# Fourier filter, routed experts and a dense block in one kernel: a weight unit every five steps, 15 leading blocks, half of the splits on GpSimd

## The chip, the cores and the metric

The kernel runs on one core of a Trainium2 chip. The metric is device time of one execution in microseconds (us). Three executions of the kernel before took 4052.21, 4054.33 and 4055.38 us; the median is 4054.33 us. Engines are named as the profile names them: PE is TensorE (matmuls; PEld are its weight loads), DVE is VectorE, ACT is ScalarE, POOL is GpSimd, SP is SyncE, which here issues DMAs. Each engine runs its own instructions in order, and semaphores tie them to each other.

## The reference

Three stages follow each other, all in fp32:

```python
X = np.fft.rfft(x, axis=1)                              # x: 8 x 3072 x 256
y = np.fft.irfft(X * (filt_r + 1j * filt_i), n=3072, axis=1)
x = y.reshape(24576, 256)
e = argmax(x @ w_gate, axis=1)                          # one of 8 experts per token
out[mask] = gate[mask] * (relu(x[mask] @ w1[e]) @ w2[e])   # 256 -> 1024 -> 256
h = out @ w_in                                          # 256 -> 2048, weights in float64
g = h if h >= 1, 0 if h <= -1, else (h + 1)**2 / 4
result = g @ w_out                                      # 2048 -> 256, weights in float64
```

To reach fp32 accuracy the matmuls of the last two stages run as three products: every operand is split into a rounded part ("hi") and the remainder ("lo"), and hi*hi, hi*lo and lo*hi are added up.

## The kernel before

The first stage (class `Conv`) transforms, filters, transforms back, writes the rows `y` to memory and routes each token to its expert. It ends at about 740 us. The other two stages are class `Ffn`, and this is where the change lies.

Tokens are gathered by expert into blocks: 41 wide blocks of 512 tokens and 21 narrow ones of 256. A block `j` has 8 parts, one step `("b", j, f)` each. A b step of a wide block is 12 matmuls on PE: six with w1 into `h` (`b_in`, L844) and, three steps later (`LAG = 3`), six with w2 into the sums `y` (`b_out`, L857). Between the two, ACT rounds `h` to `hh` and DVE computes the remainder `hl` (L854). The dense block works in chunks of 512 tokens, 16 steps `("c", c, f)` each. `run` (L986) writes all steps into one list. The first `8 * LEADERS + 12` steps are b steps alone (the lead: 13 blocks and a half); from there on, eight b steps are spread among the 16 c steps of each chunk until the wide blocks are used up. Narrow blocks are spread over every second chunk.

`plan` (L1044) sets, counted in steps ahead of a block's own step, when its work is issued: `gather` issues indirect DMAs on POOL, token numbers 26 steps ahead, rows 16 ahead (first argument of `early`, plus 7); `scale` (L825) multiplies the rows by their gate on DVE; `take` (L831) transposes one half of the rows on PE into the one PSUM bank `xt`, after which ACT copies it to `xh` and DVE writes the remainder `xl`. With `early = (9, 7, 4)` the scale stands 9 steps ahead of the block, the first half 7 and the second half 4. The second half's transposes write the bank that the first half's `xl` reads. `load_w` loads a quarter of a block's expert weights into one of three `raw` buffers, by a DMA on SP; `split_w` (L796) has ACT copy 128x512 weights to `wh`, and a step later `lo_part` (L776, the subtraction is at L778) writes the remainder `wl`. Which engine does that is decided at L801: in the lead DVE for every step, later DVE for even `f` and POOL for odd `f`.

`decode` (L738) converts the float64 weights of the dense block, 16 units of 128x512 numbers, during the last part of the lead. A unit loads `d_raw` on SP; seven DVE and two ACT instructions follow over several steps (a `yield` ends the part of a step). A new unit starts every 4 steps, and the first starts 69 steps ahead of the end of the lead. When the sums of a block are full, `b_end` (L872) has ACT copy them to `cyh` and DVE write `cyl`.

`play` (L1057) issues, for each step: the matmuls of `b_in` and the ACT half; then the remainders due (`fill`); then `hl`; then everything in `todo` for the next step (gathers, scale, transposes, loads, weight copies, decode); then `b_out` of three steps ago. Steps below are counted from the first b step, which is step 0.

Of the kernel before, what the change touches and what calls it, by code (L numbers as in the profile page):

```python
# [13 lines left out]
ACTF = mybir.ActivationFunctionType  # L14
ALU = mybir.AluOpType
# [16 lines left out]
NS = 21  # L32
NBLK = NW + NS
SURE = NBLK - 4
LEADERS = 13
WARM = 44
SPLIT_FROM = 3
NX = 7
# [647 lines left out]
class Ffn:  # L686
# [6 lines left out]
    def __init__(self, ctx, tc, a, st):  # L693
# [6 lines left out]
        self.rawp, self.wp = pool("c_raw", 3), pool("c_w", 7)  # L700
        self.idp, self.idl, self.rowp = pool("c_id", 12), pool("c_il", LEADERS), pool("c_row", 8)
        self.xp, self.hp, self.y1p, self.cyp = pool("c_x", 2), pool("c_h", 4), pool("c_y1", 1), pool("c_cy", 2)
# [35 lines left out]
    def decode(self, n):  # L738


        nc, V, pool = self.nc, self.nc.vector, self.dp
        q, k = divmod(n, 4)
        if k < 2:
            src = self.a["win"].bitcast(I32)[128 * k : 128 * k + 128, 1024 * q : 1024 * q + 1024]
            hi, lo = (t[:, k, 512 * q : 512 * q + 512] for t in (self.winh, self.winl))
        else:
            i = 4 * q + 2 * (k - 2)
            src = self.a["wout"].bitcast(I32)[128 * i : 128 * i + 256].rearrange("(t p) c -> p t c", p=128)
            hi, lo = (t[:, i : i + 2].rearrange("p t d -> p (t d)") for t in (self.woh, self.wol))
        raw = pool.tile([128, 512, 2], I32, name="d_raw")  # L750
        dst = raw.rearrange("p n w -> p (n w)")
        nc.sync.dma_start(dst if k < 2 else dst.rearrange("p (t c) -> p t c", t=2), src)
        yield
        yield
        h, l = raw[:, :, 1], raw[:, :, 0]
        e = pool.tile([128, 512], I32, name="d_e")
        m = pool.tile([128, 512], I32, name="d_m")
        f = m[:].bitcast(FP32)
        V.tensor_scalar(out=e, in0=h, scalar1=20, scalar2=0x7FF, op0=ALU.logical_shift_right, op1=ALU.bitwise_and)
        nc.scalar.activation(e, e, ACTF.Relu, bias=self.ebias[:, 0:1], scale=2.0**23)  # L760
        V.tensor_scalar(out=l, in0=l, scalar1=8, scalar2=0xFFFFFF, op0=ALU.logical_shift_right, op1=ALU.bitwise_and)
        yield
        V.tensor_scalar(out=m, in0=h, scalar1=0xFFFFF, scalar2=None, op0=ALU.bitwise_and)
        V.scalar_tensor_tensor(out=e, in0=h, scalar=-(2**31), in1=e, op0=ALU.bitwise_and, op1=ALU.bitwise_or)
        yield
        V.scalar_tensor_tensor(out=f, in0=l, scalar=2.0**-24, in1=m, op0=ALU.mult, op1=ALU.add)
        V.scalar_tensor_tensor(out=f, in0=f, scalar=2.0**20, in1=e[:].bitcast(FP32), op0=ALU.add, op1=ALU.mult)
        nc.scalar.copy(hi, f)
        yield
        self.lo_part(f, hi, lo, True)  # L770
# [14 lines left out]
    def at(self, i, fn, when=None):  # L785
        (self.todo if when is None else when).setdefault(max(i, self.now), []).append(fn)
# [9 lines left out]
    def split_w(self, j, f, i):  # L796
        q, t = divmod(f, 2)
        hi = self.wp.tile([128, 4, 128], F32R, name="wh")
        lo = self.wp.tile([128, 4, 128], F32R, name="wl")
        src = self.RAW[j, q][:, 512 * t : 512 * t + 512].rearrange("p (a b) -> p a b", b=128)  # L800
        self.halves(i, src, hi[:], lo[:], f % 2 == 0 or i < self.lead)  # L801
        self.W[j, f] = (hi, lo)

    def gather(self, j, more):
# [3 lines left out]
        if not more:  # L808
            pool, name = (self.idl, "idl") if j < LEADERS else (self.idp, "ids")
            ids = self.IDS[j] = pool.tile([128, 4, 2], I32, name=name)  # L810
# [61 lines left out]
    def b_end(self, j, acc, n):  # L872
# [4 lines left out]
        for k in range(2):  # L877
            nc.scalar.copy(hi[:, k], acc[k])
            nc.vector.tensor_tensor(out=lo[:, k], in0=acc[k], in1=hi[:, k].bitcast(FP32), op=ALU.subtract)
        if LEADERS <= j < NW:  # L880
            self.CY[j] = (hi, lo, self.rows(self.IDS.pop(j)))
# [104 lines left out]
    def run(self):  # L986
        self.now = -self.LEAD
        sure = SURE
        chunks = [*range(LEADERS, NW), *range(LEADERS), *range(NW, self.nch)]
        wide = [("b", j, f) for j in range(NW) for f in range(8)]  # L990
        narrow = [[("b", j, f) for f in range(8)] for j in range(NW, sure)]
        lead = self.lead = 8 * LEADERS + 12
        steps, wide = wide[:lead], wide[lead:]
        for m, c in enumerate(chunks):
            more, wide = wide[:8], wide[8:]
            if m >= 2 and m % 2 == 0 and narrow:
                more[4:4] = [None, *narrow.pop(0), None]
            n = max(8, len(more))
            for f in range(16):
                steps += [("c", c, f), *filter(None, more[f * n // 16 : (f + 1) * n // 16])]  # L1000
        assert not wide and not narrow
        pos = {x: i for i, x in enumerate(steps)}
        at = self.at
        fork = pos["c", self.nch - 3, 5]
        at(fork - 16, self.load_used)

        for c in range(self.nch):
            if c < LEADERS or c >= NW:
                at(pos["c", c, 0] - 7, lambda c=c: self.load_c(c))
            for t in range(4 if c < self.nch - 1 else 0):  # L1010
                at(pos["c", c, 15] + 2 + self.LAG + t, lambda c=c, t=t: self.scatter(c, t))
        for j in range(sure):
            p = [pos["b", j, f] for f in range(8)]
            if j <= LEADERS + 1:
                self.plan(p, j, soon=j == 0)
            else:
                self.plan(p, j, ahead=6, lead=8, early=(13, 11, 6))
        for n in range(16):
            d = self.decode(n)
            for k in range(7):  # L1020
                at(lead - 69 + 4 * n + k, lambda d=d: next(d, None))
        at(lead - 1, self.dense)

        for i in self.play(steps):
            if i == fork:
                self.rest(sure)
            yield i
# [13 lines left out]
                pass  # L1041
        self.todo, self.fill, self.now = keep

    def plan(self, p, j, ahead=3, lead=4, soon=0, early=(9, 7, 4)):  # L1044

        at, i = self.at, p[0] - soon
        at(p[0] - 26, lambda: self.gather(j, False))
        at(p[0] - early[0] - 7, lambda: self.gather(j, True))
        at(i - early[0], lambda: self.scale(j))
        for k in range(2):  # L1050
            at(i - early[1 + k], lambda k=k: self.take(j, k, i - early[1 + k] + 1))
        for q in range(4):
            at(p[2 * q] - ahead - lead, lambda q=q: self.load_w(j, q))
        for f in range(8):
            at(p[f] - ahead, lambda f=f: self.split_w(j, f, p[f] - ahead))
# [129 lines left out]
```

## Time and profile before

| what | value |
|---|---|
| profiled execution | 4052.3 us |
| its span in the trace | 4050.5 us |
| PE busy | 3906.5 us (96%) |
| DVE, ACT, POOL busy | 2230.3, 2006.8, 2236.0 us |
| mean granted clock of PE over the span | 0.984 of 2.4 GHz |

A share of the whole span says little here, since the kernel has stages: the first stage up to about 580 us, its tail mixed with the lead up to about 740 us, the lead with the decoded weights up to 1010.7 us, the chunks with wide blocks up to about 2950 us, and the rest. A step can be found in the trace by its six matmuls of L850; step 0 starts at 578.5 us, step 47 at 738.3 us, and the 116 steps of the lead have ended by 1010.7 us.

### The profile page before, as it was taken

What the parts mean: (1) busy time and instruction counts of PE and PEld (TensorE: products, weight loads), DVE (VectorE), ACT (ScalarE), POOL (GpSimd) and SP (SyncE); (2) the same over time, 40 slices, a digit from 0 to 9 for tenths busy, and PEclk for the clock granted to TensorE, in tenths of its full rate; (3) what the DMA queues carried; (4) which work ended last, traced back from release to release, by engine and by line L of the source; (5) the groups of instructions that cost most, each with busy time, mean ns of one, the idle gap of its engine ahead of it and who ended that gap; (6) DMA issues with size and microseconds to landing.
All of it is one profiled execution on the core that took longest, in us unless ns stands there. A gap on an engine that the chain in (4) does not pass through costs nothing. (4 is left out here: it accounts for less than half of the span.)

```text
span 4050.5 us, 63427 instructions
## 1 busy us (share of the span) xinstructions
PE 3906.5 (96%) x23852; PEld 3337.2 (82%) x23852; DVE 2230.3 (55%) x3621; ACT 2006.8 (50%) x3592; POOL 2236.0 (55%) x2112
## 2 busy tenths in 40 slices
PE   8999999888999999999999999999999999999999
PEld 5766667666888888888888888888888889888888
DVE  4577766766555554554555555555545454444444
ACT  4767654444444454444444444444444444444444
POOL 5878773211555555555555555555555555555555
PEclk9999989988999999999999999999999999999999
DMA  9878764443112221221221221221211111111010
GB/s 282 253 223 229 204 186 138 139 151 136 42 61 59 70 59 60 65 68 57 62 73 52 62 72 56 60 70 55 60 61 59 55 38 51 48 36 33 32 43 17
DMA packets 227992, 361.94 MB, mean 89 GB/s; under 512 B 35456, under 2 KB 143264, under 8 KB 227680
## 3 DMA queue, kind: packets, MB, share of 16 engines
q1 hardware_dynamic: 202400, 306.38, 24.8%
q0 software_dynamic: 25056, 51.36, 4.5%
q8 instruction: 190, 3.11, 0.3%
q14 instruction: 122, 1.00, 0.1%
q10 hardware_dynamic: 224, 0.09, 0.0%
HBM read 259.48 MB, written 98.26 MB: 88 GB/s over the span
## 5 line engine op out<-in xcount | busy, mean ns | idle before, releaser
L778 POOL TENSOR_TENSOR gl<-m,gh 128x512 fp32r<-128x512 f32 x768 | 999.1, 1301 | 1293.4 <-ACT gh L924 931.5
L921 ACT ACTIVATE m<-m,half 128x512 f32<-128x512 f32 x768 | 556.1, 724 | 951.9 <-DVE m L920 951.3
L944 PE MATMUL o<-woh,gh 128*128 128x256 f32 x3084 | 877.2, 284 | 24.7 <-ACT os L937 24.5
L944 PE MATMUL o<-woh,gl 128*128 128x256 f32 x3084 | 872.0, 283 | 5.2 <-POOL gl L778 5.2
L944 PE MATMUL o<-wol,gh 128*128 128x256 f32 x3084 | 871.4, 283 | 0.8 <-issue 0.8
L920 DVE TENSOR_SCALAR m<-h 128x512 f32<-128x512 f32 x768 | 530.5, 691 | 537.8 <-PE h L916 505.0
L923 DVE SCALAR_TENSOR_TENSOR m<-h,m 128x512 f32<-128x512 f32 x768 | 531.2, 692 | 522.1 <-ACT m L921 522.1
L924 ACT CAST gh<-m 128x512 fp32r<-128x512 f32 x768 | 476.4, 620 | 610.7 <-DVE m L923 604.8
L944 PEld LDWEIGHTS o<-woh,gh 128*128 128x128 f32 x3084 | 586.9, 190 | 61.2 <-ACT os L937 33.0
L916 PE MATMUL h<-cyh,winh 128*128 128x512 f32 x1536 | 607.7, 396 | 1.2 <-PEq L1035 1.2
L944 PEld LDWEIGHTS o<-wol,gh 128*128 128x128 f32 x3084 | 587.7, 191 | 25.4 <-issue 1.0
L916 PE MATMUL h<-cyl,winh 128*128 128x512 f32 x1536 | 608.1, 396 | 0.0
L916 PE MATMUL h<-cyh,winl 128*128 128x512 f32 x1536 | 599.2, 390 | 0.0
L944 PEld LDWEIGHTS o<-woh,gl 128*128 128x128 f32 x3084 | 587.8, 191 | 7.7 <-POOL gl L778 7.7
L854 DVE SCALAR_TENSOR_TENSOR hl<-h,hh 128x512 fp32r<-128x512 f32 (+1 forms) x464 | 284.4, 613 | 507.2 <-ACT hh L852 507.0
L916 PEld LDWEIGHTS h<-cyh,winl 128*128 128x128 f32 x1536 | 289.0, 188 | 66.8
L865 PE MATMUL y<-hh,wh 128*128 128x512 f32 (+1 forms) x928 | 343.9, 371 | 0.0
L850 PE MATMUL h<-xh,wh 128*128 128x512 f32 (+1 forms) x928 | 341.3, 368 | 1.6 <-DVE xl L778 0.8
L865 PE MATMUL y<-hl,wh 128*128 128x512 f32 (+1 forms) x928 | 341.1, 368 | 0.0
L850 PE MATMUL h<-xl,wh 128*128 128x512 f32 (+1 forms) x928 | 338.9, 365 | 0.0
L865 PE MATMUL y<-hh,wl 128*128 128x512 f32 (+1 forms) x928 | 338.1, 364 | 0.0
L850 PE MATMUL h<-xh,wl 128*128 128x512 f32 (+1 forms) x928 | 335.9, 362 | 0.0
(197 smaller groups left out, 6197.1 us busy)
## 6 DMA issues: line engine op xcount, KB each, us to landing
raw<-in_w_dram SPq DMA_DIRECT2D x232, 512.0 KB
f<-in_filt_dram SPq DMA_DIRECT2D x72, 384.0 KB
xt<-in_x_dram SPq DMA_DIRECT2D x64, 384.0 KB
s_z<-zs SPq DMA_DIRECT2D x128, 192.0 KB
zt<-s_z SPq DMA_DIRECT2D x64, 384.0 KB
s_y<-y SPq DMA_DIRECT2D x128, 192.0 KB
cyh<-s_y1h SPq DMA_DIRECT2D x20, 512.0 KB
cyl<-s_y1l SPq DMA_DIRECT2D x20, 512.0 KB
```

The source lines that it names most:

```text
L778: eng.tensor_tensor(out=lo, in0=src, in1=hi.bitcast(FP32), op=ALU.subtract)
L850: nc.tensor.matmul(o, w[:, k, :], x[:, k, :], start=i == 0, stop=i == 5)
L854: nc.vector.scalar_tensor_tensor(out=lo, in0=o, scalar=0.0, in1=hi.bitcast(FP32), op0=ALU.max, op1=ALU.subtract)
L865: nc.tensor.matmul(acc[d], w[:, 2 + d, :], x, start=(f == 0 and i == 0), stop=(f == 7 and i == 2), skip_group_check=True,)
L916: nc.tensor.matmul(ps, w[:, k, 128 * f : 128 * f + 128], x[:, k, :], start=n == 0, stop=n == 5)
L920: V.tensor_scalar(out=m, in0=ps, scalar1=-1.0, scalar2=1.0, op0=ALU.max, op1=ALU.min)
L921: nc.scalar.activation(m, m, ACTF.Square, bias=self.half[:, 0:1], scale=-0.5)
L923: V.scalar_tensor_tensor(out=m, in0=ps, scalar=-1.0, in1=m, op0=ALU.max, op1=ALU.add)
L924: nc.scalar.copy(hi, m)
L944: self.nc.tensor.matmul(self.ACC["c"][t // 2][:, t % 2, :], x[:, 128 * t : 128 * t + 128], w[:, f, :], start=(f == 0 and t % 2 == 0 and n ...
```

## The change

`LEADERS` goes from 13 to 15, so the lead grows from 116 to 132 b steps, and the chunks have 16 fewer to take in. `decode` starts a unit every 5 steps instead of 4, waits one step longer for its load, and puts one step between an instruction and the one on another engine that uses its result; the first unit starts 87 steps ahead of the end of the lead (step 45; before step 47). In the lead, too, odd `f` now has its `wl` on POOL. The default of `early` becomes (9, 8, 4), which holds for blocks 0 to 16: the first half is transposed 8 steps ahead, not 7.

```diff
-LEADERS = 13
+LEADERS = 15
...
         nc.sync.dma_start(dst if k < 2 else dst.rearrange("p (t c) -> p t c", t=2), src)
-        yield
-        yield
+        for _ in range(3):
+            yield
         h, l = raw[:, :, 1], raw[:, :, 0]
         e = pool.tile([128, 512], I32, name="d_e")
+        V.tensor_scalar(out=e, in0=h, scalar1=20, scalar2=0x7FF, op0=ALU.logical_shift_right, op1=ALU.bitwise_and)
+        V.tensor_scalar(out=l, in0=l, scalar1=8, scalar2=0xFFFFFF, op0=ALU.logical_shift_right, op1=ALU.bitwise_and)
+        yield
+        nc.scalar.activation(e, e, ACTF.Relu, bias=self.ebias[:, 0:1], scale=2.0**23)
         m = pool.tile([128, 512], I32, name="d_m")
         f = m[:].bitcast(FP32)
-        V.tensor_scalar(out=e, in0=h, scalar1=20, scalar2=0x7FF, op0=ALU.logical_shift_right, op1=ALU.bitwise_and)
-        nc.scalar.activation(e, e, ACTF.Relu, bias=self.ebias[:, 0:1], scale=2.0**23)
-        V.tensor_scalar(out=l, in0=l, scalar1=8, scalar2=0xFFFFFF, op0=ALU.logical_shift_right, op1=ALU.bitwise_and)
-        yield
         V.tensor_scalar(out=m, in0=h, scalar1=0xFFFFF, scalar2=None, op0=ALU.bitwise_and)
+        yield
         V.scalar_tensor_tensor(out=e, in0=h, scalar=-(2**31), in1=e, op0=ALU.bitwise_and, op1=ALU.bitwise_or)
-        yield
         V.scalar_tensor_tensor(out=f, in0=l, scalar=2.0**-24, in1=m, op0=ALU.mult, op1=ALU.add)
+        yield
         V.scalar_tensor_tensor(out=f, in0=f, scalar=2.0**20, in1=e[:].bitcast(FP32), op0=ALU.add, op1=ALU.mult)
+        yield
         nc.scalar.copy(hi, f)
         yield
         self.lo_part(f, hi, lo, True)
...
-        self.halves(i, src, hi[:], lo[:], f % 2 == 0 or i < self.lead)
+        self.halves(i, src, hi[:], lo[:], f % 2 == 0)
...
-            for k in range(7):
-                at(lead - 69 + 4 * n + k, lambda d=d: next(d, None))
+            for k in range(10):
+                at(lead - 87 + 5 * n + k, lambda d=d: next(d, None))
...
-    def plan(self, p, j, ahead=3, lead=4, soon=0, early=(9, 7, 4)):
+    def plan(self, p, j, ahead=3, lead=4, soon=0, early=(9, 8, 4)):
```

Three places in the order of the instructions, all in the decoding part of the lead. The first is DVE around the first half's `xl` of a block (`d_` names are those of decode, `cyl` and `y` belong to the end of the block before). Before:

```order
L854 SCALAR_TENSOR_TENSOR hl<-h,hh 128x512
L763 TENSOR_SCALAR d_m<-d_raw 128x512
L764 SCALAR_TENSOR_TENSOR d_e<-d_raw,d_e 128x512
L778 TENSOR_TENSOR wl<-raw,wh 128x512
L854 SCALAR_TENSOR_TENSOR hl<-h,hh 128x512
L766 SCALAR_TENSOR_TENSOR d_m<-d_raw,d_m 128x512
L767 SCALAR_TENSOR_TENSOR d_m<-d_m,d_e 128x512
L879 TENSOR_TENSOR cyl<-y_9249,cyh 128x512
L879 TENSOR_TENSOR cyl<-y_9250,cyh 128x512
L778 TENSOR_TENSOR xl<-xt,xh 128x512
L778 TENSOR_TENSOR wl<-raw,wh 128x512
L854 SCALAR_TENSOR_TENSOR hl<-h,hh 128x512
```

Now, at the like place of another block:

```order
L856 SCALAR_TENSOR_TENSOR hl<-h,hh 128x512
L768 SCALAR_TENSOR_TENSOR d_m<-d_m,d_e 128x512
L856 SCALAR_TENSOR_TENSOR hl<-h,hh 128x512
L780 TENSOR_TENSOR xl<-xt,xh 128x512
L780 TENSOR_TENSOR wl<-raw,wh 128x512
L856 SCALAR_TENSOR_TENSOR hl<-h,hh 128x512
L780 TENSOR_TENSOR wol<-d_m,woh 128x512
L757 TENSOR_SCALAR d_e<-d_raw 128x512
L758 TENSOR_SCALAR d_raw<-d_raw 128x512
L881 TENSOR_TENSOR cyl<-y_9505,cyh 128x512
L881 TENSOR_TENSOR cyl<-y_9506,cyh 128x512
```

The `xl` of the first half stood behind the two `cyl` and now stands ahead of them, and between two `hl` there is a `wl` in every second step alone.

The second place is ACT over one decoded unit (`woh` and `winh` are the rounded dense weights). Before:

```order
L852 ACTIVATE hh<-h 128x512
L760 ACTIVATE d_e<-d_e,ebias 128x512
L782 CAST wh<-raw 128x512
L852 ACTIVATE hh<-h 128x512
L782 CAST xh<-xt 128x512
L782 CAST wh<-raw 128x512
L852 ACTIVATE hh<-h 128x512
L768 CAST woh<-d_m 128x512
L782 CAST wh<-raw 128x512
L878 CAST cyh<-y_9249 128x512
L878 CAST cyh<-y_9250 128x512
L852 ACTIVATE hh<-h 128x512
```

Now:

```order
L854 ACTIVATE hh<-h 128x512
L760 ACTIVATE d_e<-d_e,ebias 128x512
L784 CAST wh<-raw 128x512
L854 ACTIVATE hh<-h 128x512
L784 CAST wh<-raw 128x512
L880 CAST cyh<-y_9239 128x512
L880 CAST cyh<-y_9240 128x512
L854 ACTIVATE hh<-h 128x512
L784 CAST wh<-raw 128x512
L854 ACTIVATE hh<-h 128x512
L770 CAST winh<-d_m 128x512
L784 CAST xh<-xt 128x512
```

Between the unit's first ACT instruction and its second there were two `hh`, now there are three; the DVE instruction that each waits for was issued in the same step before, and is issued one step ahead of it now.

The third place is POOL in the lead. Before:

```order
L820 DMA row<-s_y,idl 128x256 x4
L728 MEMSET ebias 128x1
L600 MEMSET one 128x128
L601 MEMSET pb 128x1
L602 MEMSET cb 128x1
L603 MEMSET Q 128x8
L813 DMA idl<-s_L,idx 128x2 x4
L820 DMA row<-s_y,idl 128x256 x4
```

Now:

```order
L815 DMA idl<-s_L,idx 128x2 x4
L780 TENSOR_TENSOR wl<-raw,wh 128x512
L822 DMA row<-s_y,idl 128x256 x4
L780 TENSOR_TENSOR wl<-raw,wh 128x512 x3
L815 DMA idl<-s_L,idx 128x2 x4
L780 TENSOR_TENSOR wl<-raw,wh 128x512
L822 DMA row<-s_y,idl 128x256 x4
```

POOL had nothing but gathers (and small memsets of the index tables) here; now the four gathers of numbers and the four of rows have one `wl` between them and three behind.

## Rows read from the trace of the kernel before

**Rows 1.** Busy time by stretch: length, busy (count) per engine, PEclk, DMA share, GB/s.

```profile
578.50:738.30 159.80, 151.51 (x750) 114.35 (x751) 111.57 (x224) 76.83 (x141) 69.72 (x69) 0.99 0.44 143
738.30:1010.70 272.40, 221.49 (x898) 175.26 (x897) 187.39 (x398) 111.60 (x204) 47.13 (x53) 0.89 0.42 142
1010.70:1085.40 74.70, 74.70 (x421) 64.86 (x420) 37.29 (x61) 34.11 (x56) 36.10 (x30) 1.00 0.13 43
```

**Rows 2.** The same view, second stretch, line 850 alone.

```profile
738.30:1010.70 272.40, 113.17 (x414) 82.16 (x414) 0.89 0.42 142
```

**Rows 3.** Waits, 738.3 to 1010.7 us: engine line <- releaser: us, times, longest.

```profile
POOL row L820 <- PE xt L838: 140.9, 7, 25.4
...
PE xt L838 <- DVE xl L778: 48.6, 8, 8.1
...
ACT d_e L760 <- DVE d_e L759: 36.6, 16, 4.0
...
ACT winh L768 <- DVE d_m L767: 28.7, 8, 5.2
```

**Rows 4.** Timeline of PE: start, us, instruction, idle before it and releaser.

```profile
841.80 0.39 PE L850 MATMUL h<-xh,wh 128*128 128x512 f32 x1
...
845.03 0.39 PE L850 MATMUL h<-xh,wh 128*128 128x512 f32 x1
...
847.83 0.39 PE L850 MATMUL h<-xh,wh 128*128 128x512 f32 x1
...
859.64 1.09 PE L838 MATMUL xt<-ident,row 128*128 128x128 f32 x4 [7.38 <-DVE xl L778]
```

**Rows 5.** Timeline of VectorE (DVE) in the same wait.

```profile
849.54 0.43 DVE L759 TENSOR_SCALAR d_e<-d_raw 128x512 int32<-128x512 int32 x1 [1.17 <-DMA d_raw<-in_wout_dram]
...
855.23 0.69 DVE L767 SCALAR_TENSOR_TENSOR d_m<-d_m,d_e 128x512 f32<-128x512 f32 x1
857.60 1.29 DVE L879 TENSOR_TENSOR cyl<-y,cyh 128x512 fp32r<-128x512 f32 x2 [1.69 <-ACT cyh L878]
858.81 0.68 DVE L778 TENSOR_TENSOR xl<-xt,xh 128x512 fp32r<-128x512 f32 x1
```

**Rows 6.** Timeline of ScalarE (ACT) in the same wait.

```profile
855.95 0.62 ACT L768 CAST woh<-d_m 128x512 fp32r<-128x512 f32 x1 [2.73 <-DVE d_m L767]
856.48 0.61 ACT L782 CAST wh<-raw 128x512 fp32r<-128x512 f32 x1
857.00 1.06 ACT L878 CAST cyh<-y 128x512 fp32r<-128x512 f32 x2
857.95 0.61 ACT L852 ACTIVATE hh<-h 128x512 fp32r<-128x512 f32 x1
```

**Rows 7.** Timeline of SyncE (SP): one issue.

```profile
845.28 0.43 SPq L752 DMA_DIRECT2D d_raw<-in_wout_dram  x1
```

**Rows 8.** Groups of DVE, 738.3 to 1010.7 us: count, busy us, mean ns, idle before.

```profile
L854 DVE SCALAR_TENSOR_TENSOR hl<-h,hh 128x512 fp32r<-128x512 f32 x70 | 48.2, 689 | 57.8 <-ACT hh L852 57.8
L778 DVE TENSOR_TENSOR wl<-raw,wh 128x512 fp32r<-128x512 f32 x67 | 45.7, 683 | 0.0
...
L767 DVE SCALAR_TENSOR_TENSOR d_m<-d_m,d_e 128x512 f32<-128x512 f32 x16 | 11.1, 692 | 0.6
...
L759 DVE TENSOR_SCALAR d_e<-d_raw 128x512 int32<-128x512 int32 x16 | 6.9, 433 | 11.7 <-DMA d_raw<-in_wout_dram 6.2 <-DMA d_raw<-in_win_dram 5.4
...
L827 DVE TENSOR_SCALAR row<-row,idl 128x256 f32<-128x256 f32 x24 | 6.8, 345 | 0.0
```

**Rows 9.** Groups of GpSimd (POOL), 1050 to 2900 us, among the chunks.

```profile
L778 POOL TENSOR_TENSOR wl<-raw,wh 128x512 fp32r<-128x512 f32 x148 | 191.6, 1295 | 0.2
...
L820 POOL DMA_INDIRECT row<-s_y,ids x124 | 118.2, 953 | 32.9 <-issue 27.0 <-ACT wh L782 3.7 <-PE h L916 0.3
```

**Rows 10.** One group of DVE in the same stretch.

```profile
L778 DVE TENSOR_TENSOR wl<-raw,wh 128x512 fp32r<-128x512 f32 x148 | 119.5, 807 | 0.0
```

**Rows 11.** Waits of PE, 2900 to 3500 us.

```profile
PE o L944 <- ACT os L937: 17.4, 10, 2.4
```

More of the change, by code (lines that the diff above doesn't have):

```diff
@@ L752, in decode @@
         nc.sync.dma_start(dst if k < 2 else dst.rearrange("p (t c) -> p t c", t=2), src)
-        yield
-        yield
+        for _ in range(3):
+            yield
         h, l = raw[:, :, 1], raw[:, :, 0]
         e = pool.tile([128, 512], I32, name="d_e")
+        V.tensor_scalar(out=e, in0=h, scalar1=20, scalar2=0x7FF, op0=ALU.logical_shift_right, op1=ALU.bitwise_and)
+        V.tensor_scalar(out=l, in0=l, scalar1=8, scalar2=0xFFFFFF, op0=ALU.logical_shift_right, op1=ALU.bitwise_and)
+        yield
+        nc.scalar.activation(e, e, ACTF.Relu, bias=self.ebias[:, 0:1], scale=2.0**23)
         m = pool.tile([128, 512], I32, name="d_m")
         f = m[:].bitcast(FP32)
-        V.tensor_scalar(out=e, in0=h, scalar1=20, scalar2=0x7FF, op0=ALU.logical_shift_right, op1=ALU.bitwise_and)
-        nc.scalar.activation(e, e, ACTF.Relu, bias=self.ebias[:, 0:1], scale=2.0**23)
-        V.tensor_scalar(out=l, in0=l, scalar1=8, scalar2=0xFFFFFF, op0=ALU.logical_shift_right, op1=ALU.bitwise_and)
+        V.tensor_scalar(out=m, in0=h, scalar1=0xFFFFF, scalar2=None, op0=ALU.bitwise_and)
         yield
-        V.tensor_scalar(out=m, in0=h, scalar1=0xFFFFF, scalar2=None, op0=ALU.bitwise_and)
         V.scalar_tensor_tensor(out=e, in0=h, scalar=-(2**31), in1=e, op0=ALU.bitwise_and, op1=ALU.bitwise_or)
+        V.scalar_tensor_tensor(out=f, in0=l, scalar=2.0**-24, in1=m, op0=ALU.mult, op1=ALU.add)
         yield
-        V.scalar_tensor_tensor(out=f, in0=l, scalar=2.0**-24, in1=m, op0=ALU.mult, op1=ALU.add)
         V.scalar_tensor_tensor(out=f, in0=f, scalar=2.0**20, in1=e[:].bitcast(FP32), op0=ALU.add, op1=ALU.mult)
+        yield
         nc.scalar.copy(hi, f)
@@ L991, in run @@
         narrow = [[("b", j, f) for f in range(8)] for j in range(NW, sure)]
-        lead = self.lead = 8 * LEADERS + 12
+        lead = 8 * LEADERS + 12
         steps, wide = wide[:lead], wide[lead:]
```

## The prediction

> **What bounds the kernel now.** I read the busy time by stretch first, then the waits of the worst stretch, then one wait on the timelines of the engines in it, and last the durations that I need for the sum.
>
> Among the chunks PE is never free: in 1010.7 to 1085.4 us it is busy for all of the 74.70 us, at a granted clock of 1.00 [rows 1]. In the stretch ahead, 738.3 to 1010.7 us, it is busy for 221.49 of 272.40 us and its clock is 0.89 in the mean [rows 1], a mix of the two levels 2.4 and 1.2 GHz. The reader is to see that both losses lie there. That stretch holds 414 matmuls of L850 [rows 2], 414 / 6 = 69 b steps. An undisturbed step takes 847.83 - 845.03 = 2.80 us; one with four transposes in it 845.03 - 841.80 = 3.23 us, so a take costs 0.43 us [rows 4]. Undisturbed, the 69 steps with their 17 takes would be 69 x 2.80 + 17 x 0.43 = 200.5 us. The excess is 272.4 - 200.5 = 71.9 us: 272.40 - 221.49 = 50.9 us in which PE stands still, and 21.0 us of matmuls at the lower clock.
>
> The waits say what it is: 48.6 of the 50.9 us are eight waits of the transposes for `xl` on DVE, the longest 8.1 us [rows 3], one per block. DVE is busy for 187.39 of 272.40 us, 69% [rows 1], so it isn't simply full. The timelines show the knot. PE waits 7.38 us until 859.64 [rows 4]. The `xl` it waits for starts at 858.81, behind two `cyl`, for which DVE had idled 1.69 us because of ACT's `cyh` [rows 5]. And `cyh` came late, at 857.00, since ACT had stood 2.73 us in front of `woh` until DVE's `d_m` of 855.23 was written [rows 5, 6]. So DVE waits for ACT and ACT for DVE, in turn, each in its own order, and the second half's transposes have one step of slack against that. Over the stretch ACT idled 36.6 us for `d_e` in 16 waits and 28.7 us for the `d_m` of eight `winh` [rows 3]; the eight `woh` are much alike.
>
> **The change, part by part.** *The step between engines.* The DVE instruction now stands a step ahead of the ACT one that reads it, so ACT finds `d_e` and `d_m` written unless DVE is a whole step late. The 16 stalls on `d_e` and the 16 on `d_m` should go. The unit keeps seven DVE instructions: four with two inputs at about 0.69 us and three at 0.43 us [rows 8], 4.04 us in all.
>
> *Five steps a unit, half of the splits on POOL.* Per block of 8 steps DVE had 8 `hl` (5.5 us), 8 `wl` (5.5), 2 units (8.1), 2 `xl` and 2 `cyl` (2.7), 4 `row` (1.4) [rows 8]: 23.2 us against PE's 8 x 2.80 + 2 x 0.43 = 23.3 us. Now it has 4 `wl` (2.7) and 1.6 units (6.5), 18.8 us. That is 81% of PE's time and leaves 4.5 us a block.
>
> *The first half a step earlier.* Its `xl` now stands ahead of the two `cyl`, with two steps instead of one before the transposes that read over it. This alone cuts the chain 857.00 to 859.49 that ended the wait. Its price: the scale is now one step ahead of the first transposes instead of two. From the end of `b_in` the chain is `hh` 0.61, `hl` 0.69, four `row` of 0.345 = 2.68 us [rows 6, 8] against a step of 2.80; whatever DVE is late beyond 0.1 us stops PE. Nothing below and 1.0 us a block above bound it; I take 0.5. Newly visible at the next step is `y`: `wh` 0.61, the first `cyh` 0.53 and the first `cyl` 0.65 (half of 1.06 and of 1.29) [rows 5, 6] make 1.8 us, against the 1.4 us of `b_in` that lie between. I take 0.4 us a block.
>
> *Two blocks more in the lead.* 16 steps and 4 takes leave the chunks, where PE is full, and run in the lead. If PE is full there too, this changes nothing. But the wide blocks end two chunks earlier, and two more changes of chunk lack their cover: there PE waits for `os`, 17.4 us in ten waits [rows 11], so 2 x 1.74 = 3.5 us. The two blocks are also written to memory and read back; their issues stand on SP seven steps ahead of use, at a DMA share of 0.13 to 0.42 [rows 1]. I cost them at nothing; late, they would cost one wait each at two chunks.
>
> *POOL.* It gets four `wl` of 1.295 us a block [rows 9] beside eight gathers of 0.95 us with 0.27 us idle ahead of each (32.9 / 124) [rows 9]: 15 of 23 us. In its order come four gathers (5.0 us), a `wl`, four gathers, three `wl`. A `wl` has about 5.6 us, two steps, from its `wh` to its matmul; behind a run of gathers it is done some 3 us before PE needs it. The gathers of rows wait for transposes (140.9 us, at most 25.4 [rows 3]), but because POOL runs ahead with nothing else to do; the transposes stand four steps earlier in the program than the gather. The `raw` buffer is now freed by POOL's `wl`, about when DVE freed it; a load issued at 845.28 [rows 7] was used at 849.54 [rows 5], 4.3 us, and has three steps (8.4 us) where it had two.
>
> What I can't see in this trace is POOL arithmetic beside decode. Among the chunks, where POOL computes, DVE's `wl` takes 807 ns [rows 10] against 683 ns in the lead [rows 8]: 0.12 us more for an instruction with two inputs from SBUF. On the lead's 43 `wl` and 64 decode instructions of that kind this is 13 us in 85 steps, within the slack of DVE. The Trainium skill, "SBUF — State Buffer", section "SBUF: two separate sides", says that GpSimd and such a DVE instruction take a common port by an exclusive lock and the loser waits for the whole of the other. The direction agrees with 807 against 683 ns; what full blocking would give is the second rival.
>
> **The sum.** The 85 steps from step 47 to the new end, with 21 takes, are 247 us undisturbed. I add 10.6 blocks x 0.9 = 9.5 us, and 5 us for the index tables, whose matmuls and DVE work stay in this stretch (the 2.3 us of idle time beside the 48.6 are theirs). Ahead of it, 578.5 to 738.3 us, PE idles 159.80 - 151.51 = 8.3 us [rows 1]; half the `wl` leave DVE there and the take is earlier too, so I take back half, 4 us. Together: -71.9 + 14.5 - 4 + 3.5 = -57.9. From the profiled execution's 4052.3 us that is 3994.4; the median of the runs lies 2.0 us above the profiled one: 3996 us. With none of the disturbances and all of the 8.3 us it is 3978; with 1.9 us more a block it is 4016.
>
> **Rivals.** *The wait only moves.* The scale one step ahead of the first transposes takes the place of `xl`, or DVE stays late since it still waits for each `hh` (57.8 us in the stretch [rows 8]). For it: the margin of 0.1 us. Against: DVE's 4.5 us a block. Half of the old price would be (48.6 + 21.0) / 8 / 2 = 4.4 us a block, 46 us over 10.6 blocks in place of the 14.5, and nothing gained ahead: 4052.3 - 71.9 + 46 + 3.5 + 2 = 4032 us.
>
> *DVE stands behind POOL.* If each of 43 `wl` on POOL holds DVE for its whole 1.295 us, that is 56 us on top of DVE's 85 steps at 18.8 / 8 = 2.35 us and about 10 us of index tables: 266 us against PE's 247, so DVE bounds the stretch, 19 us longer: 4015 us. The 0.12 us of rows 10 speaks against it.
>
> *Slower: POOL is late.* If a `wl` sits behind eight gathers in a run (10.0 us) rather than four, it ends 10.0 + 1.3 - 5.6 = 5.7 us late. In all 16.5 blocks of the lead that is 94 us: 4052.3 - 71.9 + 94 + 3.5 + 2 = 4080 us. It decides from (71.9 - 3.5) / 16.5 = 4.1 us of lateness a block. For it: 25.4 us waits in front of a gather [rows 3]. Against: the order, with a `wl` between the fours.
>
> **How the numbers follow.** The forecast has 0.72 (3978 to 4016, its own range), the moved wait 0.13, DVE behind POOL 0.08, late POOL 0.07. From 3978 to 4032 the range holds nearly all of the forecast, all of the second rival and half of the first, about 8 in 10. A change within 0.2%, 8 us, can't be told from none by a few runs of this kernel: faster by more 0.91, same 0.03, slower 0.06 (late POOL, less the mildest of it).
>
> **What would show it.** Right: from step 47 on b steps of 2.80 to 2.85 us in the mean, a clock near 1.00 in that stretch, no wait of `xt` for `xl` over 2 us, ACT's waits for `d_e` and `d_m` under 10 us together, the lead's end near 738 - 4 + 247 + 14.5 = 996 us. Short waits of the first transposes on `row`, of `y` on `cyl`, would show the residue. Wrong: waits of PE or of its weight loads on POOL's `wl`; DVE's decode instructions far over 0.69 us; or eight or more waits of 3 us and over that remain.

## The result, and the profile after

The changed kernel takes 4011.17 us (median of 4 runs, 4009.19 to 4014.26); the kernel before, on the same chip, 4054.86 us (4 runs). The ratio is 0.9894, with a 95% interval of 0.9877 to 0.9911: 43.7 us less, where 58 were forecast. The time lies inside the range and inside the forecast's own 3978 to 4016, 15 us above the predicted 3996.

The profiled execution took 4014.26 us, its span is 4012.3 us. These are its stretches, cut at the same steps as [rows 1]: step 0, step 47 and the first chunk (length, busy time and count of PE, PEld, DVE, ACT, POOL, then PEclk, DMA share, GB/s).

```profile
585.30:741.60 156.30, 153.63 (x739) 113.63 (x740) 107.38 (x196) 74.83 (x138) 92.49 (x84) 0.99 0.46 147
741.60:1009.40 267.80, 256.24 (x1105) 199.99 (x1104) 218.31 (x404) 140.74 (x244) 133.49 (x118) 1.00 0.51 172
```

The matmuls of L852 (L850 before) in the second stretch, as in [rows 2]:

```profile
741.60:1009.40 267.80, 132.94 (x510) 95.55 (x510) 1.00 0.51 172
```

510 / 6 = 85 steps, as the prediction had it, against 69 of before in about the same time. PE is busy for 256.24 of 267.80 us and its granted clock is 1.00; before it was 221.49 of 272.40 us at 0.89 [rows 1]. The undisturbed 85 steps would be 247 us, so the excess is 20.8 us where it was 71.9. The waits of that stretch (engine line <- releaser: us, times, longest):

```profile
PE xt L840 <- DVE row L829: 5.8, 7, 1.7
...
PE y L867 <- DVE cyl L881: 4.9, 9, 1.7
ACT winh L770 <- DVE d_m L768: 4.7, 4, 2.3
...
ACT d_e L760 <- DVE d_e L757: 1.6, 1, 1.6
```

The reader is to see what is gone and what is new. The transposes' waits for `xl`, 48.6 us in [rows 3], don't occur at all. ACT's 36.6 us in front of `d_e` are 1.6 us, its 28.7 us in front of `winh`'s `d_m` 4.7 us. New are the two small waits that the prediction named: the transposes for the scale (`row`) and `y` for `cyl`. No wait of PE or of its weight loads names POOL's `wl`. What DVE's instructions take there (count, busy us, mean ns, idle before):

```profile
L780 DVE TENSOR_TENSOR wl<-raw,wh 128x512 fp32r<-128x512 f32 x41 | 41.1, 1004 | 0.0
L766 DVE SCALAR_TENSOR_TENSOR d_m<-d_raw,d_m 128x512 f32<-128x512 int32 x16 | 14.3, 891 | 0.0
...
L757 DVE TENSOR_SCALAR d_e<-d_raw 128x512 int32<-128x512 int32 x16 | 10.1, 631 | 0.0
```

`wl` takes 1004 ns where it took 683, `d_e` 631 where it took 433 [rows 8]: in the mean these instructions of DVE are longer beside POOL's. E6 shows that the mean hides two kinds.

Cutting the two spans at the same steps shows where the forecast and the time part. Up to step 47 the kernel is 741.6 - 738.3 = 3.3 us later, not 4 us earlier. The decoding stretch is 267.8 us, not 261.5. Behind it 4012.3 - 1009.4 = 3002.9 us remain, against 4050.5 - 1010.7 = 3039.8: 36.9 us less, where 16 steps and 4 takes (46.7 us) less two changes of chunk (3.5 us), 43.2 us, were forecast. So three places are short, by 7.3, 6.3 and 6.3 us. The experiments look for each.

### The profile page after: what moved, and what is told of

It reads as the page before. It is cut to its first block, busy times and chain, and to the rows that moved or that the text cites. A ratio compares the mean times of both kernels' runs of the same rounds, so it can differ in the third digit from the quotient of the medians.

```text
span 4012.3 us, 63578 instructions
## 1 busy us (share of the span) xinstructions
PE 3905.1 (97%) x23852; PEld 3318.2 (83%) x23852; DVE 2238.2 (56%) x3563; ACT 2014.3 (50%) x3592; POOL 2321.0 (58%) x2170
## 5 line engine op out<-in xcount | busy, mean ns | idle before, releaser
L780 POOL TENSOR_TENSOR wl<-raw,wh 128x512 fp32r<-128x512 f32 x232 | 307.2, 1324 | 150.0 <-ACT wh L784 144.5
L852 PE MATMUL h<-xh,wh 128*128 128x512 f32 (+1 forms) x928 | 338.9, 365 | 2.4 <-DVE hl L856 1.3
L852 PE MATMUL h<-xh,wl 128*128 128x512 f32 (+1 forms) x928 | 336.1, 362 | 0.0
L852 PE MATMUL h<-xl,wh 128*128 128x512 f32 (+1 forms) x928 | 335.9, 362 | 0.0
```

The lines of the kernel that those rows point to most:

```text
L780: eng.tensor_tensor(out=lo, in0=src, in1=hi.bitcast(FP32), op=ALU.subtract)
L852: nc.tensor.matmul(o, w[:, k, :], x[:, k, :], start=i == 0, stop=i == 5)
```

## The experiments

They ran in three groups (E1 to E4, E5 to E8, F1 to F4), each on a chip of its own with the kernel before beside it: 4082.8, 4083.3 and 4072.3 us in the median. Totals are compared as ratios to that; inside the kernels, the stretches between the same steps are compared. Four executions with the same decoding part (the changed kernel, E1, E3, F1) give 267.8, 269.3, 268.9 and 269.3 us for it, so a difference of 4 us there counts; the experiments whose lead has 132 steps are held against these. Where PE waits more the stretch is less steady: the kernel before and E2, the same program but for two unused buffers, give 272.4 and 279.8 us on two chips. The ratios of E3, F1 and the first measurement, which should be all but alike, are 0.9861, 0.9884 and 0.9894, so a total decides little below 0.003 between chips.

**E1 and E2: two unused buffers.** In the chunks alone the changed kernel is slower though no instruction there has changed. The `idl` pool has grown by two tiles of 32 bytes; the program's addresses show that `cyh`, `cyl`, `xh`, `hh`, `m` and `os`, allocated behind it, started at multiples of 128 bytes and now start 64 bytes off one.

```diff
# E1, on the changed kernel; E2 is the same edit on the kernel before
-pool("c_il", LEADERS)
+pool("c_il", LEADERS + 2)
```

> The changed kernel with two more buffers in the pool of token numbers (17 in place of 15), which nothing uses: the tiles allocated behind it (cyh, cyl, xh, xl, hh, hl, row, m, os) move by 64 bytes and start at a multiple of 128 bytes again, as in the kernel before; in the changed kernel they start 64 bytes off. Theory (address): the matmul h<-cyh,winl, 228 ns to the next one before and 233 ns in the changed kernel, goes back to about 228; the dense-only chunk from 46.30 us to about 46.10; 4011 us becomes about 4001 to 4005. Rival (the pace belongs to the execution, its clock or the order of the chunks): the chunk stays at 46.3 us and the time within 3 us of 4011.

> The kernel before with 15 buffers in the pool of token numbers in place of 13, two of them unused: the same tiles move 64 bytes off a multiple of 128, as in the changed kernel, and nothing else changes. Theory (address): dense-only chunks take 46.3 us in place of 46.1, h<-cyh,winl 233 ns in place of 228, and the time rises by 7 to 10 us, to about 4063. Rival (order of the chunks or the execution): chunk and time as before, 4052 to 4057 us.

The copies of `os` come once a chunk; in the part with dense chunks alone their first and last starts give the length of a chunk. Before, changed, E1 and E2, in this order:

```profile
L937 ACT COPY os<-o x4: 579/579/579, 3538.4 to 3676.7; 128x512 f32<-128x512 f32 x4
```

```profile
L939 ACT COPY os<-o x4: 579/579/579, 3498.0 to 3636.9; 128x512 f32<-128x512 f32 x4
```

```profile
L939 ACT COPY os<-o x4: 578/578/578, 3508.0 to 3646.3; 128x512 f32<-128x512 f32 x4
```

```profile
L937 ACT COPY os<-o x3: 579/579/579, 3522.8 to 3615.4; 128x512 f32<-128x512 f32 x3
```

(3676.7 - 3538.4) / 3 = 46.10 us before; (3636.9 - 3498.0) / 3 = 46.30 changed; (3646.3 - 3508.0) / 3 = 46.10 with the pad; (3615.4 - 3522.8) / 2 = 46.30 with the kernel before moved. The pace follows the addresses in both directions. From the first chunk to the last matmul it makes 2991.7 us in E1 against 2998.0 in the changed kernel, and 3041.8 us in E2 against 3035.3: 6.3 and 6.5 us. That is the third shortfall. The single matmul is not so plain: `h<-cyh,winl` to the next takes 228 ns before and 233 changed, as expected, but 241 in E1, where others got faster. The totals are 0.9843 (0.9829 to 0.9857) for E1 and 1.0006 (0.9997 to 1.0014) for E2. E1 bears the reading out: on the same chip E3 below, which lacks the two buffers (and takes block 0 a step later), takes 6.6 us more in the median, and their runs don't overlap. E2 does not: its interval ends at 5.7 us, below the 6.5 of the trace and the 7 to 10 that I expected. What came back ahead of the chunks is not known, since the kernel before has no profile on that chip.

**E3 and E4: step 0 and the scale.** In the changed kernel step 0 starts at 585.3 us, before at 578.5. The waits of PE between 540 and 600 us, changed and before:

```profile
PE h L840 <- DVE row L829: 10.4, 5, 5.6
```

```profile
PE h L838 <- DVE row L827: 5.3, 3, 2.9
```

The transposes of the first blocks wait for rows that come no earlier.

```diff
# E3
-                self.plan(p, j, soon=j == 0)
+                self.plan(p, j, soon=j == 0, early=(9, 7 if j == 0 else 8, 4))
# E4
-    def plan(self, p, j, ahead=3, lead=4, soon=0, early=(9, 8, 4)):
+    def plan(self, p, j, ahead=3, lead=4, soon=0, early=(10, 8, 4)):
```

> The changed kernel with the first half of block 0 alone taken 7 steps ahead again; blocks 1 to 16 keep 8. Theory (the rows of the first blocks aren't there yet, so the earlier transposes stop PE, 5.6 us in one wait at 566 us, with the clock at half after it, and step 0 starts at 585.3 in place of 578.5 us): the longest wait for row is back at about 3 us, step 0 starts 4 to 7 us earlier, the time is about 4005 us. Rival (the rows themselves are late, or step 0 is late because of the splits on GpSimd): step 0 stays within 2 us of 585 and the time within 3 us of 4011.

> The changed kernel with scale and row gather one step earlier (10, 8, 4): the scale stands two steps ahead of the first transposes again, and the rows are asked for 17 steps ahead. Theory (what is left in the lead is in part the scale, 5.8 us of waits of the matmuls xt for row and 5.5 us of weight loads there): the waits of xt for row go, 20.8 us of excess in the lead become about 12 to 15, the time falls by 5 to 8 us to about 4004 to 4006. Rival (the remaining waits are those of y for cyl and take their place): the time stays within 3 us of 4011.

Neither did what I expected. With E3, step 0 starts 11.2 us after the first transposes, as in E1 (586.3 to 597.5 there), so block 0 isn't what holds it: ratio 0.9861 (0.9846 to 0.9877). With E4 the distance is 8.2 us, and the waits of `xt` for `row` are gone, but others grew: `y` waits 10.3 us where it was 4.9, the stretch takes 273.9 us, 5 us more, and steps 0 to 47 take 165.5 us instead of 156 to 157. Ratio 0.9883 (0.9866 to 0.9899). So the scale's 1.4 us of DVE [rows 8] were not saved; that they were moved to where `hl` and `cyl` need DVE is argued from these waits.

**E5 to E7: one edit undone at a time.**

```diff
# E5: the old take times
-early=(9, 8, 4)):
+early=(9, 7, 4)):
# E6: all splits of the lead on DVE (run sets self.lead)
-lo[:], f % 2 == 0)
+lo[:], f % 2 == 0 or i < self.lead)
# E7: no step between engines (the length of a unit is kept)
         V.tensor_scalar(out=e, in0=h, ...)
+        nc.scalar.activation(e, e, ACTF.Relu, ...)
         V.tensor_scalar(out=l, in0=l, ...)
         yield
-        nc.scalar.activation(e, e, ACTF.Relu, ...)
...
+        yield
         V.scalar_tensor_tensor(out=f, in0=f, ...)
-        yield
         nc.scalar.copy(hi, f)
```

> The changed kernel with the old take times (9, 7, 4) and everything else new. Theory (the knot was DVE and ACT waiting for each other, and the load on DVE): waits of the second half's transposes for xl come back in small, 1 to 2.5 us in each of some 10 blocks, since cyl stands ahead of xl again; the time is 4015 to 4030 us. Rival (the earlier take is what did it): waits of 5 us and over per block return and the time is 4045 or more.

> The changed kernel with all splits of the lead on DVE again, everything else new. Theory (DVE has 21.5 us of work a block against PE's 23.3 us without this part): the lead is disturbed a little more, 1 to 3 us a block, 4015 to 4035 us. Rival (the load on DVE was the cause): DVE is late throughout, waits of 5 us a block return, 4045 us or more. A third way: no worse than the changed kernel, 4005 to 4012 us, if DVE's slack is enough.

> The changed kernel with the step between engines taken out of decode: the ACT instruction stands again in the same step as the DVE instruction it reads, a unit keeps its five-step spacing and its length. Theory (DVE and ACT waiting for each other was the larger part): ACT waits again about 1.8 to 2.3 us at each of 32 places, hh and cyh are late behind it, the lead loses 15 to 40 us, 4025 to 4050 us. Rival (spacing, splits and the take's time suffice): 4009 to 4016 us.

The ratios are 0.9902 (0.9885 to 0.9918), 0.9879 (0.9862 to 0.9895) and 0.9893 (0.9877 to 0.9910), which by themselves can't be told from the changed kernel's 0.9884 and 0.9894 on other chips. The stretches tell more. E5:

```profile
PE xt L840 <- DVE xl L780: 22.9, 10, 4.0
...
ACT d_e L760 <- DVE d_e L757: 3.1, 4, 1.2
```

The waits for `xl` are back in ten blocks at 2.3 us in the mean, while ACT waits 3.1 us for `d_e` and 6.0 us for the `d_m` of `winh`: the size that the theory gave. The decoding stretch takes 280.6 us, 12 more, and steps 0 to 47 another 8 to 9 (165.3 us). E7:

```profile
ACT d_e L758 <- DVE d_e L757: 33.1, 16, 3.5
...
PE y L867 <- DVE cyl L881: 14.4, 10, 2.2
ACT woh L770 <- DVE d_m L769: 12.8, 7, 3.3
```

ACT's 33.1 us in front of `d_e` are back, at 16 places, and `y`, which hangs on ACT's `cyh`, waits 14.4 us where it waited 4.9. The stretch takes 282.1 us, 13 to 14 more. E6:

```profile
749.40:1024.50 275.10, 261.43 (x1105) 204.34 (x1104) 213.43 (x448) 140.24 (x246) 65.18 (x69) 0.97 0.49 168
```

The stretch takes 275.1 us, 6 to 7 more. But DVE's busy time is 213.43 us with 84 `wl`, and 218.31 in the changed kernel with 41: the work that went to POOL came back as longer instructions, `wl` at 682 ns in the mean here and 1004 there. Their shortest, median and longest ns, in E6 and in the changed kernel:

```profile
L780 DVE TENSOR_TENSOR wl<-raw,wh x84: 671/682/725, 749.5 to 1016.5; 128x512 fp32r<-128x512 f32 x84
```

```profile
L780 DVE TENSOR_TENSOR wl<-raw,wh x41: 673/682/2184, 745.7 to 999.1; 128x512 fp32r<-128x512 f32 x41
```

The median didn't move. In the changed kernel 29 of DVE's `wl` take 0.67 to 0.69 us as ever; the other 12 take 1.21 to 2.18 us, and each of these overlaps a `wl` of POOL and ends 0.55 to 0.56 us after it.

**E8: thirteen blocks and four steps a unit.**

```diff
-LEADERS = 15
+LEADERS = 13
...
-                at(lead - 87 + 5 * n + k, lambda d=d: next(d, None))
+                at(lead - 72 + 4 * n + k, lambda d=d: next(d, None))
```

> The changed kernel with 13 leading blocks and a unit every four steps again (first unit at step 44); the step between engines, the splits on GpSimd and the take times stay new. Theory (spacing matters less than the knot: DVE has 20.4 us of work a block against 23.3): excess of the lead like that of the changed kernel or a few us more over fewer blocks, two chunk changes of 1.7 us saved, tiles on multiples of 128 bytes again, so 4000 to 4015 us. Rival (five steps are needed): 4025 us or more.

```profile
750.40:971.90 221.50, 211.82 (x897) 165.58 (x896) 187.98 (x365) 118.84 (x204) 105.46 (x94) 0.98 0.49 174
```

PE waits 7.2 us for `row` and 2.3 us for `cyl`. The 69 steps take 221.5 us, an excess of 21.0 us over 200.5, as much as the changed kernel has over its 85. So neither the wider spacing nor the two blocks was needed. Behind the lead E8 takes 3035.3 us, as before. Decoding stretch and rest together are 3256.8 us against 267.8 + 2998.0 = 3265.8: 9.0 us less, about the 6.3 of the addresses and the 3.5 of the two changes of chunk. The ratio is 0.9837 (0.9821 to 0.9854), 4013.6 us on a chip where the kernel before takes 4083.3. E5 to E7 ran on that chip too. With the 9.0 us put back, the changed kernel would take about 4022.6 us there, an estimate; E5, E6 and E7 lie 19, 8 and 17 us above it. Their stretches and steps 0 to 47 together (165.3, 158.1 and 157.3 us for the latter) are about 20, 8 and 14 us longer than the changed kernel's, so the totals agree with the stretches.

**F1 to F4: the changed kernel again, and two edits on E8.**

```diff
# F2, on E8
+                self.plan(p, j, soon=j == 0, early=(9, 7 if j < 2 else 8, 4))
# F3, on E8: a block's sums are copied ahead of the next weights
+            first = self.LAG <= i < min(self.lead, n) and steps[i - self.LAG][::2] == ("b", 7)
+            if first:
+                self.b_out(steps[i - 3][1], 7)
             go(todo, i + 1)
...
```

F4 has both edits.

> The changed kernel itself once more, on the chip of the experiments, where the kernel before takes about 4083 us. Theory (address and blocks 0 and 1): 6 us above the padded one, so a ratio to the kernel before of 0.985 to 0.987, 4023 to 4030 us. Rival (the first measurement holds here too): 0.9894, 4040 us.

> The kernel with 13 leading blocks and four steps a unit, with the first half of blocks 0 and 1 taken 7 steps ahead again (blocks 2 and up: 8). Theory (it is block 1 whose transposes now stand ahead of step 0 and wait for its rows): the time from the first transposes to step 0 falls from 11 to 8 us, the whole by 2 to 4 us: ratio 0.9828 to 0.9832. Rival (step 0 is late, but the time comes back behind it): ratio within 0.0005 of 0.9837.

> The kernel with 13 leading blocks and four steps a unit; in the lead, ACT's copies of a block's sums to cyh stand ahead of the next weight copy wh instead of behind it (the order on PE is the same). Theory (what is left at y is the chain wh, cyh, cyl, 1.8 us against 1.4): the waits of y for cyl, 2.3 us on PE, go, and the ratio falls by 0.0003 to 0.001. Rival (the transposes, which wait for row, take it up): within 0.0004 of 0.9837.

> The two edits above together. Theory: they add up, ratio 0.982 to 0.983, 4 to 6 us below the kernel with 13 leading blocks and four steps a unit, the best so far. Rival: no more than the better of the two.

F1 gives 0.9884 (0.9870 to 0.9898) with 4022.8 us: with the first measurement's 0.9894 that is the changed kernel; the 0.985 to 0.987 that I had reckoned from E1 and E3 on another chip doesn't hold. F2, F3 and F4 give 0.9849 (0.9836 to 0.9862), 0.9845 (0.9833 to 0.9858) and 0.9840 (0.9828 to 0.9853), 4009.9, 4007.6 and 4006.1 us. All three lie below F1 on the same chip; between themselves and E8 no difference can be told.

In F2 PE's wait for the rows ahead of step 0 falls to 0.2 us (F1: 1.3), and step 0 starts at 588.8 against 591.9 us; in F4, where the edit stands beside F3's, it starts at 590.4, as in F3 alone (590.5), but there the second transposes of block 0 stand 2.6 us later (587.0 against 584.4). Counted from these, step 0 follows after 3.3 us in F2 and 3.7 us in F4, against 6.4 us in F1 and F3. The other groups agree: 3.7 to 3.9 us where block 1 is taken 7 steps ahead (E2, E5), 6.4 to 7.4 us where it is 8 (E1, E3, E6 to E8), 4.6 us in E4, which asks for the rows a step earlier. So block 1 holds step 0, by about 3 us. Steps 0 to 47 take 1.2 us more with it (F4's 155.7 against F3's 154.5; F2 has 156.9), and in the totals no gain shows.

In F3 `y` waits 1.0 us where it waits 2.6 in F2 on the same chip, but `xt` waits 8.0 us for `row` instead of 6.9: the next in line takes most of it.

## Why the prediction was right, and where it was short

**The knot.** Right, in place and kind. The eight waits of 48.6 us are gone, with them the lower clock of that stretch, and undoing either half of it brings back its own waits: E5 those for `xl`, E7 those of ACT for DVE. Undone one at a time, take times, step between engines and splits cost 12, 13 and 6 us of the stretch (against 268.8, the mean of the four), 31 together. All undone at once, in the kernel before, cost 51 us (71.9 against 20.8), and 57 by E2 on a chip of the experiments:

```profile
757.10:1036.90 279.80, 223.36 (x898) 175.94 (x897) 187.54 (x398) 111.50 (x204) 47.58 (x53) 0.87 0.41 139
```

That is 279.8 - 200.5 = 79.3 us of excess, against 268.8 - 247 = 21.8. So the three partly stand in for each other. The 6 us of the splits are the least sure, one execution each and less than the 7.4 us between the kernel before and E2.

**The residue of the lead.** The mechanism was right, the size short: 20.8 us for 14.5. The prediction gave the scale 0.5 and `y` 0.4 us a block; in the records PE waits 5.8 us for `row` and 4.9 for `cyl` in 10.6 blocks, which is just that, and 0.8 us for the index tables. The remaining 9 us are no idle time in the records. Cutting the stretch at every step's first matmul places them. Of the 84 steps that lie wholly in it, 64 hold no transposes and take 179.4 us, 2.80 each, as forecast. 18 hold the four transposes of a take, 75.1 us with 10.1 us of idle time, so 3.61 us each without it, where 3.23 were reckoned: 6.9 us. Two hold matmuls of the index tables too, 10.5 us with 1.4 of idle time: 2.6 us above 3.23 each. One step with a take, 0.16 us of it idle:

```profile
835.15 0.40 PE L852 MATMUL h<-xh,wh 128*128 128x512 f32 x1
...
838.82 0.39 PE L852 MATMUL h<-xh,wh 128*128 128x512 f32 x1
```

So the term that was mis-sized is the take: 0.81 us, not the 0.43 us that I read in a single place where PE waited for nothing [rows 4]. Of the 18 only one (3.23 us) costs that; why the others cost more stays open. The forecast sign of 2.80 to 2.85 us a step holds for the 64 steps. For all of them, less takes of 0.43 us, it is (267.8 - 9.0) / 85 = 3.04 us; but the forecast's own 261.5 us would make 2.97, so the sign left out the residue that the sum had.

**DVE behind POOL.** The step that went most wrong in kind. I took 0.12 us for a DVE instruction with two inputs from the chunks [rows 10]; beside POOL's `wl` in the lead it was 0.32 us on `wl` and 0.21 on L766, and the three instructions with one input, which I had left at 0.43, took up to 0.63. Over 41 `wl` and 16 units this is about 26 us, not 13. The price was a mean over two kinds. In the chunks 24 of the 148 `wl` took 1.18 to 1.50 us and the others 0.68; in the lead it was 12 of 41, at 1.79 us. So the rival's mechanism, DVE held until POOL's instruction is done, did occur, but for 12 `wl` of 41 and not for each; what the chunks could not tell was how often they would meet. It stayed inside DVE's slack, as forecast, so the rival's bound was not reached, but it is why the edit that was to relieve DVE by 2.7 us a block took nothing off its busy time, though the stretch is 6 us shorter with it.

**The stretch ahead.** Forecast 4 us gained, measured 3.3 us lost. Steps 0 to 47 did gain 3.5 us (156.3 against 159.8), close to the 4; on the chip of E1 and E2 it was 9.8 us (157.3 against 167.1). But step 0 starts 6.8 us later, and the sum had no term for that. The first gather of rows, which the change didn't move, already starts 4.1 us later than before:

```profile
561.56 0.95 POOL L820 DMA_INDIRECT row<-s_y,idl  x1 [0.30 <-issue]
```

```profile
565.67 0.94 POOL L822 DMA_INDIRECT row<-s_y,idl  x1 [0.30 <-issue]
```

That is not the change's doing: in the 14 traces of this case POOL's first gather starts anywhere from 546.5 to 555.3 us, in this one last of all, and at 549.8 us in the same kernel run again (F1). What the prediction overlooked is that the take times also hold for block 1, whose first transposes now stand ahead of step 0: step 0 follows the second transposes of block 0 after 5.2 us, before after 3.7, so 1.5 us here and about 3 us in the experiments. The last 1.2 us stay open.

**Behind the lead.** The two changes of chunk cost what was forecast (PE's waits for `os` are 12 between 2850 and 3460 us, at 1.7 us each, where they were ten). The 6.3 us that are missing are the addresses (E1, E2), a cost that no term of the sum had: two small tiles more in one pool.

**The rivals.** The wait did move to the scale, but with 5.8 us in place of 48.6. POOL was late nowhere: its `wl` ended 3.2 us or more ahead of the matmul that reads it, 5.3 us or more from the third one on. The prediction's own reckoning was at odds there, since with its 5.6 us a `wl` behind four gathers would end 5.0 + 1.3 - 5.6 = 0.7 us late, not 3 us early; in the trace a `wl` had more time than that.

## What to carry to other kernels

When two engines with their own queues hand one piece of work back and forth, put a step between the hand-overs before you make more room: the engine that was busy for 69% held PE up because of whom it waited for, and the wider spacing and the two leading blocks that went with it turned out to be needed for nothing, at 3.5 us for the two blocks. Before work is moved to relieve an engine, compare that engine's busy time after the move, not only its count of instructions, and when a mean has grown, look at the shortest and the longest one. And when a pool grows, look at the addresses of what is allocated behind it.

## What the runs showed of the hardware

The same matmuls at the same clock of 1.00 run 0.4% slower (46.30 against 46.10 us a chunk) when the operands start 64 bytes off a multiple of 128: seen in two pairs of kernels, and the chunks of every other kernel here fall on its side of it (E8 and F2 to F4 46.10; E3 to E7 and F1 46.30). Which of the moved tiles does it was not separated. Why single matmuls shift among each other (228, 233 and 241 ns for the same one) stays open.

Most of DVE's instructions that read SBUF alone grew beside POOL's arithmetic, in the mean by up to a half: `wl` from 682 ns (E6) to 1004 ns, L766 from 686 to 891, `d_e` from 422 to 631. `winl` and `wol`, which started first in each of their five meetings, kept their 0.68 us. Nor did the others grow evenly: the 12 long `wl` overlap a `wl` of POOL and end 0.55 us behind it, the 29 others take their 0.68 us. In the five meetings in which DVE's `wl` kept its 0.68 us, POOL's took 1.32 to 1.84 us, and in the mean POOL's own `wl` went from 1295 [rows 9] to 1360 ns. `hl` and `xl`, which read PSUM, met POOL's `wl` eight and six times and took 0.68 to 0.69 us each time. This is what the Trainium skill, "SBUF — State Buffer", section "SBUF: two separate sides", says of a lock held for the whole instruction, and the 12 long `wl` agree with it. That instructions with one input grew as well (three of the 16 `d_e` took 1.53 to 1.54 us, the others 0.42 in the mean) agrees with the Trainium skill, "SBUF — State Buffer", section "Who interferes with whom", which counts their faster mode among what takes the common port; in which mode they ran no trace here shows. And the Trainium skill, "Perfetto Trace Analysis", section "Optimizing Scalar/DVE Operations", warns that moving work between those two might not help: the busy times of E6 and of the changed kernel, 213.43 and 218.31 us, agree with that.
